# Three edits to the routed-expert stage of a one-core Trainium2 kernel: exchanged arms of a branch, another output place, an earlier split of inputs

## The chip, the cores and the metric

The kernel runs on one NeuronCore of a Trainium2 chip. The metric is device time in microseconds. The profiler's record of one execution is the trace read below. Engines are named as in the profile: PE (TensorE, matrix products), DVE (VectorE), ACT (ScalarE), POOL (GpSimd) and SP (the queue that issues most loads). Each engine runs its own list of instructions in order and waits on semaphores for the others.

## The reference, cut to what matters

Local and global attention gives 2176 rows of 512 numbers. A feed-forward stage with a squared relu follows, and then a stage of routed experts, the only one that the change touches:

```python
do_compute = x @ w_skip > 0
xc = x[do_compute]
e_idx = np.argmax(xc @ w_gate, axis=1)         # one of 8 experts
for e in range(E):                             # F = 1024, D = 512
    mask = e_idx == e
    h = np.maximum(xc[mask] @ w1[e], 0.0)
    y[mask] = gate_w[mask, None] * (h @ w2[e])
out[do_compute] = xc + y                       # other rows stay x
```

For the input that is timed, the experts 0 to 7 get 337, 24, 22, 433, 82, 126, 86 and 133 rows.

## The kernel before

Every float32 product is done as three products of a high and a low half (fp32r): weights and inputs are each split, the high half by ACT (a cast), the low half by DVE (a subtraction, line 846 for weights). In names like `e34h` and `e34l` the number is 8 times the expert plus the part of its weights, so `e32` to `e39` are expert 4's and `e40` to `e47` expert 5's.

The rows of one expert are worked in tiles of 128 (`expert_tile`), in eight steps with a `yield` after each: four of the first product (relu goes to `er`, is transposed and split into `ehl`), four of the second (into `y`), then the output `eo` on DVE (line 1061: gate times y plus x), then an indirect DMA on POOL that scatters the rows to `out` (line 1065). Inputs come by an indirect gather on POOL (`gather`, line 990), are transposed on PE (`etr`) and split (`prepare`).

How many tiles an expert has is known only at run time. Expert e's tile 0 always runs. Behind it, `more(e, 1)` holds further tiles under branches (line 1384). Experts 1 and 2 have so few rows here that they go together through a small path, and then `run(range(3, 8))` does experts 3 to 7. For expert 3 there is one question more: if its count needs exactly seven half tiles, the 305 rows behind tile 0 go through `wide_tile`, one tile of 320 columns, and otherwise through `more(3, 1)`. `prepare_wide` makes its inputs in three pieces (`etr_1w` to `etr_3w`, low halves on line 925), its first product is in lines 937 to 939, its outputs are transposed back (line 976), formed on DVE (line 982, three tiles `ewo`, `ewo` and `xg_wide`) and scattered on POOL (`scatter_rest`, line 1132). The other inputs of this run take the path so far described: expert 3 tile 0 and the wide tile, experts 4, 5 and 6 one tile each, expert 7 one tile and a rest of 32 rows.

The order on every engine is the order in which the code emits instructions. `run` calls `work(e, u)` after step u of expert e: it converts the next expert's weights by the table `PARTS_AT`, five parts ahead, issues loads of later weights, and by `AHEAD` two gathers, that of expert e+2's tile 0 after step 2 and that of expert e+1's further tile after step 3. `prepare(e, 1)` stands after step U1 = 5 and `prepare(e + 1, 0)` after step U0 = 6, whether or not the further tile turns out to be needed. Both scatter and gather go through POOL in program order, and a scatter to `out` waits for the scatter before it.

Places in SBUF go by tags. "xt" has one buffer: all `eo` tiles use it, and so do the first of the wide tile's outputs and the outputs of the small paths. "vgr" has one buffer, too, for values that attention reads; the expert stage did not use it. A new tile of a tag waits until all readers of the last one, a scatter among them, are done.

A branch can have a hint: `mark_branch_hint_location`, called after step 0 of the expert's tile 0, tells PE ahead whether the branch will be taken.

Of the kernel before, what the change touches and what calls it, by code (L numbers as in the profile page):

```python
# [54 lines left out]
def attention_ffn_routed_experts(  # L55
# [24 lines left out]
    SG = q_g.shape[2]  # L80
    P = 128
# [20 lines left out]
    BLK = 2 * P  # L102
# [12 lines left out]
    def sb(tag, bufs, shape, name, dtype=F32):  # L115
        return spool.tile(shape, dtype, tag=tag, bufs=bufs, name=name + arm[0])
# [267 lines left out]
    def load_v_global(b, g):  # L384
        h0 = 4 * g
        vgl[b, g] = stage(f"gv{b}_{g}").rearrange("p (h j d) -> p h j d", h=4, j=TPB)
        nc.sync.dma_start(vgl[b, g], v_l[b, h0:h0 + 4].rearrange("h (p j) d -> p h j d", j=TPB))
        if g == 0:
            vgr[b] = sb("vgr", 1, [SG, DM], f"vgr{b}")
            nc.sync.dma_start(heads(vgr[b]), v_g[b].rearrange("h s d -> s h d"))  # L390

    def attention(t, S_TAG, O_TAG):
# [416 lines left out]
    BEHIND = 5  # L809
    AHEAD = {2: ((2, 0),), 3: ((1, 1),)}  # L810
    PARTS_AT = {0: (0, 1), 1: (2,), 2: (3,), 3: (4,), 4: (5,), 5: (6,), 6: (7,)}
    U0, U1 = 6, 5
    FEW, AFTER = (1, 2), 3
    WIDE = 2 * P + P // 2
    raws, spare, shared = {}, [], {}
# [98 lines left out]
    def prepare_wide(e, j):  # L914

        n = P // 2 if j == 3 else P
        cols = slice((j - 1) * P, (j - 1) * P + n)
        tr = pair(f"etr_{e}_{j}w")
        transposes(tr, wide_x[e] if j == 3 else gathered(e, j), n)
        high, low = ([x[:, :, cols] for x in xs] for xs in wide_slices())  # L920
        for z in range(2):
            nc.scalar.copy(high[z], tr[:, 2 * z:2 * z + 2, 0:n])
        for l, h, k in ((low[0], high[0][:, 0:1], 0), (low[1], high[0][:, 1:2], 1), (low[2], high[1], 2)):
            w = l.shape[1]
            nc.vector.tensor_tensor(out=l, in0=tr[:, k:k + w, 0:n], in1=h.bitcast(F32), op=ALU.subtract)
# [82 lines left out]
    def expert_tile(e, j, si):  # L1008
# [48 lines left out]
        yield  # L1057
        second(6, KE)
        yield
        o = sb("xt", 1, [P, 3 * BLK], f"eo_{name}")[:, 0:DM]  # L1060
        nc.vector.scalar_tensor_tensor(
            out=o, in0=y, scalar=xg[:, DM:DM + 1], in1=xg[:, 0:DM], op0=ALU.mult, op1=ALU.add
        )
# [119 lines left out]
    with tc.manual_schedule():  # L1183
# [237 lines left out]
        def run(experts, later=(), ahead=NST - 1, late=U0):  # L1421
            later = list(later)
            for e in experts:
                for u, _ in enumerate(expert_tile(e, 0, slot(sidx, e, 0))):
                    if u in HINTS:
                        if is_wide(e):
                            tc.mark_branch_hint_location(f"wide{e}", hint=wide_count(e), engines=HINTS[u])
                        else:
                            hint(e, 1, HINTS[u])
                    if is_wide(e):  # L1430
                        if U1 <= u < U1 + 3:
                            prepare_wide(e, u - U1 + 1)
                    elif u == U1:
                        prepare(e, 1)
                        if e == E - 1:
                            prepare_rest(e, 1)
                    if u == (U0 if e != experts[0] else late) and e + 1 < E:
                        prepare(e + 1, 0)
                    work(e, u, ahead if e == experts[0] else NST - 1)
                    if later:  # L1440
                        later.pop(0)()
                if is_wide(e):
                    with tc.If(wide_count(e), label=f"wide{e}") as wide:  # L1443
                        wide_tile(e)
                    with wide.Else():
                        more(e, 1)
                else:
                    more(e, 1)

        def wide_count(e):  # L1450
            return (n_tok[e] + (P // 2 - 1)) // (P // 2) == 7

        more(0, 2)
        carried = dict(est), dict(raws)
# [78 lines left out]
```

## Time and profile before

| what | us |
|---|---|
| runs of the kernel before | 719.21, 726.43, 726.79 (median 726.43) |
| profiled execution | 724.18 |
| its span | 722.5 |
| PE busy in the span | 687.0 (95%) |
| DVE, ACT, POOL busy | 398.3, 368.7, 167.3 |
| expert 3, tile 0 on PE | 602.25 to 615.25 |
| wide tile on PE | 616.25 to 646.43 |
| experts 4, 5, 6, 7 on PE, first matmul | 649.43, 664.31, 681.25, 695.99 |
| rest of expert 7, first matmul | 709.15 |

The span is the profiled execution without its start and end. In rows of the timeline a number in square brackets is the time in which the engine stood idle before the instruction, with the name of what released it; a matmul's row gives its modelled length, so that the distance of two starts tells the pace. [...]

### The profile page before, as it was taken

To read this page: it belongs to the slowest core of one execution; us is meant where nothing else is said; L and a number is where in the kernel's file an instruction comes from. 1 tells how busy PE (TensorE), PEld (TensorE's weight loads), DVE (VectorE), ACT (ScalarE), POOL (GpSimd) and SP (SyncE) were. 2 spreads that over 40 slices of the span, in tenths; PEclk is the share of its full clock that TensorE was granted. 3 is DMA by queue.
4 is the path that set the end of the run, shared out by engine and by line. 5 is a ranking of instruction groups with operands and counts; after the bars stand their busy time and mean duration, and the time that the engine had idled before them with its cause. 6 is when DMAs were issued, how large, how long until landed. Compare 5 with 4: busy or idle time off the path is not lost. (4 is left out here: it accounts for less than half of the span.)

```text
span 722.5 us, 18733 instructions
## 1 busy us (share of the span) xinstructions
PE 687.0 (95%) x7617; PEld 576.4 (80%) x7617; DVE 398.3 (55%) x1073; ACT 368.7 (51%) x944; POOL 167.3 (23%) x209
## 2 busy tenths in 40 slices
PE   6789998999999999999999999999999999989995
PEld 4566677898888988988888898888878878987773
DVE  1889955763654265365245355525277428336882
ACT  5757567665534645544455363544345226226670
POOL 5000043472112221122112221122204235003211
PEclk8699999999999999999999999999999999999998
DMA  9999653064054304124620404010058599807800
GB/s 273 250 284 292 217 130 62 2 166 85 2 144 118 78 32 84 32 61 84 147 49 32 106 2 155 5 59 32 29 171 267 178 345 371 312 16 234 312 28 21
DMA packets 119096, 95.16 MB, mean 132 GB/s; under 512 B 84853, under 2 KB 92021, under 8 KB 118980
## 3 DMA queue, kind: packets, MB, share of 16 engines
q1 hardware_dynamic: 108352, 71.01, 34.9%
q10 hardware_dynamic: 8292, 15.48, 6.5%
q0 software_dynamic: 2336, 7.14, 2.9%
q8 instruction: 70, 1.15, 0.7%
q14 instruction: 46, 0.38, 0.2%
HBM read 81.36 MB, written 12.66 MB: 130 GB/s over the span
## 5 line engine op out<-in xcount | busy, mean ns | idle before, releaser
L184 POOL TENSOR_TENSOR gl<-g,gh 128x256 fp32r<-128x256 f32 x107 | 79.5, 743 | 302.6 <-ACT gh L183 153.6
L700 PE MATMUL h<-xh,w_in 128*128 128x256 f32 x464 | 134.8, 291 | 0.7 <-ACT xh L183 0.7
L701 PE MATMUL h<-xl,w_in 128*128 128x256 f32 x464 | 129.5, 279 | 0.3 <-DVE xl L184 0.3
L702 PE MATMUL h<-xh,w_in 128*128 128x256 f32 x464 | 129.7, 279 | 0.0
L725 PE MATMUL acc<-w_out,gh 128*128 128x512 f32 x232 | 97.6, 421 | 1.5 <-ACT gh L183 1.5
L727 PE MATMUL acc<-w_out,gl 128*128 128x512 f32 x232 | 91.8, 396 | 0.2
L726 PE MATMUL acc<-w_out,gh 128*128 128x512 f32 x232 | 91.6, 395 | 0.0
L700 PEld LDWEIGHTS h<-xh,w_in 128*128 128x128 f32 x464 | 87.1, 188 | 4.2 <-ACT xh L183 0.9
L701 PEld LDWEIGHTS h<-xl,w_in 128*128 128x128 f32 x464 | 87.2, 188 | 2.6 <-DVE xl L184 0.5
L704 ACT ACTIVATE g<-h 128x256 f32<-128x256 f32 x128 | 48.7, 381 | 77.0 <-PE h L702 45.1
L702 PEld LDWEIGHTS h<-xh,w_in 128*128 128x128 f32 x464 | 87.1, 188 | 0.0
L433 ACT ACTIVATE sm<-sm,mx 128x128 f32<-128x128 f32 x120 | 46.7, 390 | 50.1 <-DVE mx L431 50.1
L741 DVE TENSOR_TENSOR g<-h,g 128x256 f32<-128x256 f32 x53 | 22.2, 419 | 85.4 <-ACT g L704 85.3
L183 ACT CAST gh<-g 128x256 fp32r<-128x256 f32 x116 | 47.2, 407 | 42.8 <-DVE g L741 40.0
L727 PEld LDWEIGHTS acc<-w_out,gl 128*128 128x128 f32 x232 | 43.5, 188 | 11.9 <-POOL gl L184 1.5
L725 PEld LDWEIGHTS acc<-w_out,gh 128*128 128x128 f32 x232 | 43.6, 188 | 8.5 <-ACT gh L183 1.9
L726 PEld LDWEIGHTS acc<-w_out,gh 128*128 128x128 f32 x232 | 43.8, 189 | 5.7
L426 DVE TENSOR_TENSOR sm<-sc,mask 128x512 f32<-128x512 f32 x30 | 20.6, 687 | 24.2 <-PE sc L413 23.4
L255 POOL TENSOR_TENSOR w_in<-st_raw_in,w_in 128x512 fp32r<-128x512 f32 x10 | 13.0, 1308 | 81.4 <-ACT w_in L251 81.4
L413 PEld LDWEIGHTS sc<-kT,qT 64*32 64x32 f32 x2048 | 24.9, 108 | 5.2 <-issue 4.3
L990 POOL DMA_INDIRECT xg<-x2d,slots x15 | 20.6, 1371 | 36.5 <-DVE slots L800 13.1
L743 ACT ACTIVATE g<-g 128x256 f32<-128x256 f32 x63 | 26.2, 416 | 4.7 <-ACT g L704 2.5
(690 smaller groups left out, 1481.3 us busy)
## 6 DMA issues: line engine op xcount, KB each, us to landing
st_e<-in_moe_w_dram SPq DMA_DIRECT2D x46, 512.0 KB, 6.3
vr<-in_v_l_dram SPq DMA_DIRECT2D x49, 192.0 KB, 4.1
st_raw_in<-in_moe_w_in_dram SPq DMA_DIRECT2D x16, 512.0 KB, 7.1
st_raw_out<-in_moe_w_out_dram SPq DMA_DIRECT2D x16, 512.0 KB, 7.3
st_e<-in_moe_w_dram ACTq DMA_DIRECT2D x12, 512.0 KB, 5.4
x2d<-x ACTq DMA_DIRECT2D x19, 256.5 KB, 3.7
st_gv<-in_v_l_dram SPq DMA_DIRECT2D x8, 512.0 KB, 4.4
out_dram<-x ACTq DMA_DIRECT2D x16, 256.0 KB, 4.0
```

What stands on the lines that cost most here:

```text
L183: nc.scalar.copy(hi, src)
L184: (lo_engine or nc.vector).tensor_tensor(out=lo, in0=src, in1=hi.bitcast(F32), op=ALU.subtract)
L413: nc.tensor.matmul(scs[g][SEG * i:SEG * (i + 1), p, cols], lhsT=q[rows, p, SEG * i:SEG * (i + 1)], rhs=kT[b][rows, p, keys], start=True, s ...
L433: nc.scalar.activation(sm[:, hh, :], sm[:, hh, :], AF.Exp, bias=mx[:, hh:hh + 1], scale=SCALE, accum_out=osum[:, 2 * hh + g:2 * hh + g + 1],)
L700: nc.tensor.matmul(h, lhsT=wh, rhs=xh[:, k, :], start=(k == 0), stop=False)
L701: nc.tensor.matmul(h, lhsT=wh, rhs=xl[:, k, :], start=False, stop=False)
L702: nc.tensor.matmul(h, lhsT=wl, rhs=xh[:, k, :], start=False, stop=(k == KD - 1))
L704: nc.scalar.activation(g, h, AF.Relu)
L725: nc.tensor.matmul(acc[z], lhsT=gh[:, c], rhs=wh, start=first_one, stop=False)
L726: nc.tensor.matmul(acc[z], lhsT=gh[:, c], rhs=wl, start=False, stop=False)
L727: nc.tensor.matmul(acc[z], lhsT=gl[:, c], rhs=wh, start=False, stop=last_one)
L743: nc.scalar.activation(square, g, AF.Square)
```

## The change

It has three parts. The place of an expert's output: tile 0 of each expert puts it into the tag "vgr", which is allocated with 128 rows for that, and further tiles stay on "xt". The arms of expert 3's question: the question is turned round (`other_count`), so that `more(3, 1)` is the first arm and the wide tile the last; the hint is turned round with it. The preparation of the wide tile's inputs: it stands after the steps 4, 5 and 6 of expert 3's tile 0 instead of 5, 6 and 7.

```diff
--- before.py
+++ after.py
@@ -386,7 +386,7 @@
         vgl[b, g] = stage(f"gv{b}_{g}").rearrange("p (h j d) -> p h j d", h=4, j=TPB)
         nc.sync.dma_start(vgl[b, g], v_l[b, h0:h0 + 4].rearrange("h (p j) d -> p h j d", j=TPB))
         if g == 0:
-            vgr[b] = sb("vgr", 1, [SG, DM], f"vgr{b}")
+            vgr[b] = sb("vgr", 1, [P, DM], f"vgr{b}")[0:SG]
             nc.sync.dma_start(heads(vgr[b]), v_g[b].rearrange("h s d -> s h d"))
 
     def attention(t, S_TAG, O_TAG):
@@ -809,7 +809,7 @@
     BEHIND = 5
     AHEAD = {2: ((2, 0),), 3: ((1, 1),)}
     PARTS_AT = {0: (0, 1), 1: (2,), 2: (3,), 3: (4,), 4: (5,), 5: (6,), 6: (7,)}
-    U0, U1 = 6, 5
+    U0, U1, U2 = 6, 5, 4
     FEW, AFTER = (1, 2), 3
     WIDE = 2 * P + P // 2
     raws, spare, shared = {}, [], {}
@@ -1057,7 +1057,10 @@
         yield
         second(6, KE)
         yield
-        o = sb("xt", 1, [P, 3 * BLK], f"eo_{name}")[:, 0:DM]
+        if j:
+            o = sb("xt", 1, [P, 3 * BLK], f"eo_{name}")[:, 0:DM]
+        else:
+            o = sb("vgr", 1, [P, DM], f"eo_{name}")
         nc.vector.scalar_tensor_tensor(
             out=o, in0=y, scalar=xg[:, DM:DM + 1], in1=xg[:, 0:DM], op0=ALU.mult, op1=ALU.add
         )
@@ -1424,12 +1427,12 @@
                 for u, _ in enumerate(expert_tile(e, 0, slot(sidx, e, 0))):
                     if u in HINTS:
                         if is_wide(e):
-                            tc.mark_branch_hint_location(f"wide{e}", hint=wide_count(e), engines=HINTS[u])
+                            tc.mark_branch_hint_location(f"other{e}", hint=other_count(e), engines=HINTS[u])
                         else:
                             hint(e, 1, HINTS[u])
                     if is_wide(e):
-                        if U1 <= u < U1 + 3:
-                            prepare_wide(e, u - U1 + 1)
+                        if U2 <= u < U2 + 3:
+                            prepare_wide(e, u - U2 + 1)
                     elif u == U1:
                         prepare(e, 1)
                         if e == E - 1:
@@ -1440,15 +1443,15 @@
                     if later:
                         later.pop(0)()
                 if is_wide(e):
-                    with tc.If(wide_count(e), label=f"wide{e}") as wide:
+                    with tc.If(other_count(e), label=f"other{e}") as other:
+                        more(e, 1)
+                    with other.Else():
                         wide_tile(e)
-                    with wide.Else():
-                        more(e, 1)
                 else:
                     more(e, 1)
 
-        def wide_count(e):
-            return (n_tok[e] + (P // 2 - 1)) // (P // 2) == 7
+        def other_count(e):
+            return (n_tok[e] + (P // 2 - 1)) // (P // 2) != 7
 
         more(0, 2)
         carried = dict(est), dict(raws)
```

In the program, on PE, at the end of the wide arm (`ewtr` are its output transposes, `eh_1` further tiles of expert 3, `eh_0` with `e32h` expert 4), before:

```order
L976 MATMUL ewtr_1_a<-ident,ewys_a 128x128
L976 MATMUL ewtr_2_a<-ident,ewys_a 64x128
L1443 UNCONDITIONAL_BRANCH
L1384 COMPARE_AND_BRANCH
L1023 MATMUL eh_1_0_a<-e24h_a,xp_0_8022 128x512
L1024 MATMUL eh_1_0_a<-e24l_a,xp_0_8022 128x512
```

and in the change:

```order
L976 MATMUL ewtr_1_a<-ident,ewys_a 128x128
L976 MATMUL ewtr_2_a<-ident,ewys_a 64x128
L1446 UNCONDITIONAL_BRANCH
L1023 MATMUL eh_0_0_a<-e32h_a,xp_0_8020 128x512
L1024 MATMUL eh_0_0_a<-e32l_a,xp_0_8020 128x512
```

The wide arm lay before the block of `more(3, 1)`, and its unconditional branch jumped over that block to expert 4. Now expert 4 stands directly behind the branch. On PE the wide arm has 205 instructions in either program, and the other arm with its branch 365.

On PE, at the entry of the arms, behind the last product of expert 3's tile 0 (`etr_3w` and `etr_0_a` are transposes of the wide tile's last inputs and of expert 4's), before:

```order
L1040 MATMUL y_0_a<-e31h_a,ehl_0_a 128x512
L280 MATMUL etr_3w_a<-ident,xg_wide_a 128x64 x4
L280 MATMUL etr_0_a<-ident,xg_1_8016 128x128 x4
L1443 COMPARE_AND_BRANCH
L937 MATMUL ewh_0_a<-xp_0_8022,e24h_a 128x320
L938 MATMUL ewh_0_a<-xp_0_8022,e24h_a 128x320
L939 MATMUL ewh_0_a<-xp_0_8022,e24l_a 128x320
```

and in the change:

```order
L1039 MATMUL y_0_a<-e31l_a,ehl_0_a 128x512
L1040 MATMUL y_0_a<-e31h_a,ehl_0_a 128x512
L280 MATMUL etr_0_a<-ident,xg_1_8016 128x128 x4
L1446 COMPARE_AND_BRANCH
L1387 COMPARE_AND_BRANCH
L1023 MATMUL eh_1_0_a<-e24h_a,xp_0_8022 128x512
L1024 MATMUL eh_1_0_a<-e24l_a,xp_0_8022 128x512
```

Before, the wide tile (line 937) follows the branch; now `more(3, 1)` does, and the branch jumps over it to the wide tile. The transposes `etr_3w` have moved to a place ahead of the six matmuls of the last step.

On DVE, in the last steps of expert 3's tile 0 (`e31l` is the last part of expert 3's weights, `e32l` and `e33l` the first of expert 4's, `xp` the low halves of the wide tile's inputs), the piece of the difference between both programs, - for before and + for the change:

```order
-L846 TENSOR_TENSOR e31l_a<-st_e_8077,e31h_a 128x1024 [waits DMAHW0_49,DVE_49]
 L925 TENSOR_TENSOR xp_0_8022<-etr_1w_a,xp_0_8022 128x128 [waits PE_49,Activation_49]
 L925 TENSOR_TENSOR xp_0_8023<-etr_1w_a,xp_0_8022 128x128
 L925 TENSOR_TENSOR xp_1_8024<-etr_1w_a,xp_0_8023 128x2x128
-L846 TENSOR_TENSOR e32l_a<-st_e_8093,e32h_a 128x1024 [waits DMAHW1_49,DVE_49,Pool_49]
+L846 TENSOR_TENSOR e31l_a<-st_e_8077,e31h_a 128x1024 [waits DMAHW0_49,DVE_49]
 L925 TENSOR_TENSOR xp_0_8022<-etr_2w_a,xp_0_8022 128x128 [waits PE_49,Activation_49]
 L925 TENSOR_TENSOR xp_0_8023<-etr_2w_a,xp_0_8022 128x128
 L925 TENSOR_TENSOR xp_1_8024<-etr_2w_a,xp_0_8023 128x2x128
-L846 TENSOR_TENSOR e33l_a<-st_e_8232,e33h_a 128x1024 [waits DMAHW2_49,DVE_49]
+L846 TENSOR_TENSOR e32l_a<-st_e_8093,e32h_a 128x1024 [waits DMAHW1_49,DVE_49,Pool_49]
 L925 TENSOR_TENSOR xp_0_8022<-etr_3w_a,xp_0_8022 128x64 [waits PE_49,Activation_49]
```

Each group of three subtractions on line 925 stands one weight conversion sooner.

On DVE, at the output of expert 4's tile 0 (`eo_0_a`, read from `xg_1_8016`), with the queues that it waits for, before:

```order
L846 TENSOR_TENSOR e40l_a<-st_e_8174,e40h_a 128x1024 [waits DMAHW1_49]
L184 TENSOR_TENSOR xp_1_8021<-etr_0_a,xp_1_8021 128x512 [waits Activation_49]
L846 TENSOR_TENSOR e41l_a<-st_e_8381,e41h_a 128x1024 [waits DMAHW2_49]
L1061 SCALAR_TENSOR_TENSOR eo_0_a<-y_0_a,xg_1_8016 128x512 [waits DMASW3_49,DMASW4_49,DMASW2_49,DMASW5_49,DMASW1_49,DMASW7_49,DVE_49,PE_49]
L1384 COMPARE_AND_BRANCH
```

and in the change:

```order
L846 TENSOR_TENSOR e40l_a<-st_e_8174,e40h_a 128x1024 [waits DMAHW1_49]
L184 TENSOR_TENSOR xp_1_8021<-etr_0_a,xp_1_8021 128x512 [waits Activation_49]
L846 TENSOR_TENSOR e41l_a<-st_e_8381,e41h_a 128x1024 [waits DMAHW2_49]
L1064 SCALAR_TENSOR_TENSOR eo_0_a<-y_0_a,xg_1_8016 128x512 [waits DMASW5_49,DMASW1_49,PE_49]
L1387 COMPARE_AND_BRANCH
```

The waits for the queues DMASW3, DMASW4, DMASW2 and DMASW7, which carry the scatters of what lay in "xt", are gone; those for DMASW5, its own gather, and DMASW1 stay. On the path that runs here, the order of the scatters and gathers on POOL and their waits for one another are the same in both programs.

## Rows read from the trace of the kernel before

**Rows 1.** Page, its first line

```profile
span 722.5 us, 18733 instructions
```

**Rows 2.** Busy time by stretch, all engines; columns in the first line

```profile
core 0: us, PE busy (x) PEld busy (x) DVE busy (x) ACT busy (x) POOL busy (x), PEclk, DMA share, GB/s
649.43:653.00 3.57, 3.57 (x9) 2.79 (x10) 2.28 (x3) 0.00 (x0) 1.77 (x1) 0.52 0.61 184
664.30:681.25 16.95, 14.99 (x64) 11.66 (x65) 12.68 (x14) 11.20 (x15) 4.65 (x5) 0.90 0.94 315
...
695.99:709.15 13.16, 13.16 (x65) 10.43 (x65) 9.30 (x10) 7.82 (x11) 1.02 (x1) 1.00 0.06 18
```

**Rows 3.** PE's timeline at the wide tile's entry: start, us, instruction [idle <- releaser]

```profile
616.25 0.38 PE L937 MATMUL ewh_a<-xp,e24h_a 128*128 128x320 f32 x1
616.92 0.41 PE L938 MATMUL ewh_a<-xp,e24h_a 128*128 128x320 f32 x1 [0.29 <-DVE xp L925]
```

**Rows 4.** PE's timeline at the wide tile's exit

```profile
644.81 0.31 PE L958 MATMUL ewy_a<-ewgl_a,e31h_a 128*128 128x320 f32 x1
644.96 1.47 PE L976 MATMUL ewtr_a<-ident,ewys_a 128*128 128x128 f32 x12
649.43 0.73 PE L1023 MATMUL eh_a<-e32h_a,xp 128*128 128x512 f32 x1 [3.00 <-issue]
...
652.95 0.40 PE L1025 MATMUL eh_a<-e33h_a,xp 128*128 128x512 f32 x1
```

**Rows 5.** Branches on PE's sequencer by line: ns min/median/max, first and last start

```profile
L1443 PEldq COMPARE_BRANCH  x2: 83/1912/3742, 615.7 to 645.6; - x2
...
L1384 PEldq COMPARE_BRANCH  x7: 95/384/3751, 579.8 to 706.6; - x7
...
L1384 PEldq COMPARE_BRANCH  x1: 195/195/195, 593.1 to 593.1; - x1
```

**Rows 6.** PE's timeline in expert 5

```profile
664.31 0.47 PE L1023 MATMUL eh_a<-e40h_a,xp 128*128 128x512 f32 x1
...
666.25 0.40 PE L1025 MATMUL eh_a<-e41h_a,xp 128*128 128x512 f32 x1
...
669.38 0.50 PE L1024 MATMUL eh_a<-e42l_a,xp 128*128 128x512 f32 x1 [1.80 <-DVE e42l_a L846]
```

**Rows 7.** DVE's timeline behind the wide tile, in expert 5 and in expert 6

```profile
648.23 1.21 DVE L846 TENSOR_TENSOR e34l_a<-st_e,e34h_a 128x1024 fp32r<-128x1024 f32 x1
...
667.04 0.75 DVE L1061 SCALAR_TENSOR_TENSOR eo_a<-y_a,xg 128x512 f32<-128x512 f32 x1 [1.79 <-DMA out_dram<-xg_wide_a,slots]
668.10 1.23 DVE L846 TENSOR_TENSOR e42l_a<-st_e,e42h_a 128x1024 fp32r<-128x1024 f32 x1 [0.31 <-ACT er_a L1028]
...
683.16 1.23 DVE L846 TENSOR_TENSOR e50l_a<-st_e,e50h_a 128x1024 fp32r<-128x1024 f32 x1 [0.31 <-DVEq L1384]
```

**Rows 8.** POOL's timeline behind the wide tile

```profile
647.28 1.00 POOL L1132 DMA_INDIRECT out_dram<-ewo_a,slots  x1 [28.11 <-DVE ewo_a L982]
650.80 1.77 POOL L1132 DMA_INDIRECT out_dram<-ewo_a,slots  x1 [2.52 <-DVE e35l_a L846]
660.85 1.51 POOL L1132 DMA_INDIRECT out_dram<-xg_wide_a,slots  x1 [8.28 <-DVE ehl_a L184]
...
664.64 1.51 POOL L990 DMA_INDIRECT xg<-x2d,slots  x1 [0.30 <-issue]
```

**Rows 9.** DMA issues of two short windows (660.85, 664.64): us to landing last

```profile
out_dram<-xg_wide_a,slots POOLq DMA_INDIRECT x1, 5.9
...
xg<-x2d,slots POOLq DMA_INDIRECT x1, 7.9
```

**Rows 10.** PE's timeline in expert 6 and at expert 7's start

```profile
681.25 0.47 PE L1023 MATMUL eh_a<-e48h_a,xp 128*128 128x512 f32 x1
...
690.75 0.60 PE L280 MATMUL etr_a<-ident,xg 128*128 128x128 f32 x4
...
695.99 0.47 PE L1023 MATMUL eh_a<-e56h_a,xp 128*128 128x512 f32 x1 [1.42 <-PEq L1384]
```

## The prediction

> **What bounds the kernel now.** I read the page first: the span is 722.5 us [rows 1], and TensorE (PE) is busy for 95% of it, so only what makes PE stand still or run slowly can move the time. The profiled execution took 724.18 us, 1.7 us of it outside the span. The runs shown have a median of 726.43 and differ among themselves by 1%, so about 1% is what a measurement of this kernel can tell from no change. My sum is made against 724.18, which is 0.3% under that median and close to the mean of the numbers shown.
>
> Then I read PE's timeline around the lines of the diff, where PE loses time in three places.
>
> First, the exit of the wide tile. The last transposes end at 644.96 + 1.47 = 646.43 and the next matmul, expert 4's first, begins at 649.43: 3.00 us idle that no data explains [rows 4]. The branch of line 1443 at the end of the arm took PE's sequencer 3742 ns [rows 5]. It jumps over the whole block of the other arm, and no hint was given for it. [...]
>
> Second, inside expert 5. PE waits 1.80 us at 669.38 for `e42l` [rows 6]. VectorE (DVE) made it late because its previous instruction, expert 4's output on line 1061, had itself stood 1.79 us until the scatter of `xg_wide` landed [rows 7]: that output lies in the place "xt", like the wide tile's first output, and the wait takes in the wide tile's scatters. The clock falls again: 0.90 over the expert, which takes 16.95 us against 13.16 for expert 7 [rows 2]. Of these 3.79 us, I take 0.2 for the passage to the next expert, which stays, and 0.1 for the small wait that expert 6 has too; 3.5 hangs on the late `e42l`.
>
> Third, the entry of the wide tile. Its second matmul begins 0.67 us after its first, with 0.29 idle until the low half of the inputs is there [rows 3]; such matmuls otherwise stand 0.15 apart, as from 644.81 to 644.96 [rows 4]. That is 0.52 lost.
>
> **The change, part by part.**
>
> *Arms exchanged.* The wide arm now lies directly in front of expert 4, and its last branch goes to the next instruction. A short jump of an arm in this trace took 195 ns [rows 5]; the present exit hides 3.74 - 3.00 = 0.74 us because the sequencer runs ahead of PE, so what stays costs between 0 and 0.2; I take 0. The idle 3.00 and the slow 1.58 behind it go: 4.55, rounded. Is the data there so early? Expert 4's first half needs nothing new. The second needs `e34l`, which DVE makes from 648.23 behind the wide tile's outputs, for 1.21 us [rows 7]; with 0.5 less at the wide tile's entry it ends at 648.95. PE, starting at about 646.0, wants it 13 matmuls later at some 0.24 each, near 649. So 0 to 0.3 of a new wait; I take 0.
>
> The same exchange moves the price to the entry: what fell through now jumps over the other expert tiles. This jump has its hint, set one expert tile earlier. Of the seven branches of line 1384 on PE the median took 384 ns and only the longest 3751 [rows 5]; that one, in front of expert 7, had been hinted as well and left 1.42 us of idle time [rows 10] at full clock [rows 2]. At the wide tile's entry the sequencer is at the branch at 615.7 [rows 5] and the first matmul starts at 616.25 [rows 3]: a lead of 0.55. A hinted jump of 0.4 us fits into it: 0. A missed one shows 3.75 - 0.55 = 3.2 us as idle time, and with the 1.58 of the slow clock behind such a gap costs 4.8; were the lead that in front of expert 7, 1.42. I take 0, since the middle of these rows is a hit.
>
> [...]
>
> *An output place of its own.* Expert 4's output no longer waits for the wide tile's scatters, only for its own inputs and for expert 3's scatter, landed long ago. `e42l` then stands as in expert 6, where `e50l` began 683.16 - 681.25 = 1.91 us after the expert's first matmul instead of 668.10 - 664.31 = 3.79 [rows 6, 7, 10]. All 3.5 us go. Bounds: 3.3 (idle and slow clock without the small rests) to 3.8 (the whole difference). At expert 0's tiles and at the end of the kernel nothing waited for "xt", so nothing is gained there; the place "vgr" was last read by attention, long before.
>
> *Inputs split one step sooner.* Each of the three preparations moves up by one step, so on PE, ScalarE and DVE the same transposes, copies and subtractions stand in front of one weight conversion instead of behind it. The last low half is done about a micro-second sooner; the 0.52 at the entry goes. In exchange `e31l` to `e33l` each come up to 0.8 us later, but `e31l` is wanted behind two more groups of matmuls. Between 0 and 0.52 I take 0.5.
>
> *What is late next.* GpSimd (POOL) issues the wide tile's three scatters one after the other, each when the one before has landed: issues at 647.3, 650.80, 660.85 [rows 8]. Behind them in its program stand the two gathers of expert 4's steps, the second of which fetches the rows for expert 5's further tile: issued at 664.64 [rows 8], under way for 7.9 us [rows 9], so landed at 672.54. Nothing of that is changed but the start, 0.5 us sooner: it lands at 672.0. Were the scatters and gathers slowed by loads that come denser, it would be up to 1 us later; `xg_wide` took 5.9 [rows 9] with loads running already.
>
> PE wants these rows at expert 5's transposes. In expert 6 the same step stands at 690.75 - 681.25 = 9.50 us [rows 10]. Before, with its 3.5 us of losses, expert 5 came there at 664.31 + 9.50 + 3.5 = 677.3, far behind the landing; hence no wait shows today. After the change expert 5 starts at 664.31 - 4.55 - 0.5 = 659.26 and comes there at 668.76. PE stands 672.04 - 668.76 = 3.28 us. Its transposes are in program order ahead of the second half of expert 5's second product; on DVE and ScalarE the copies of these inputs hold up the later conversions equally, so nothing fills the gap. Both longer idle times of this trace (3.00 and 1.80) were followed by the 0.5 clock, the 1.42 was not [rows 2, 4, 6, 10]; so another 1.58 as above. This wait costs 4.85; bounds 0 (if the rows land 3.3 us sooner) and 5.8.
>
> Sum: -4.55 - 3.5 - 0.5 + 4.85 = -3.7, and 724.18 - 3.7 = **720.5 us**, 0.5% less. One can say it as a cap: whatever PE saves behind the wide tile, it cannot pass expert 5's transposes before 672.0 instead of 677.3, and pays 1.58 for standing there.
>
> **Rivals.**
>
> 1. *The new wait does not come.* The gather would have to land by 668.8. For it: the first scatter landed within 3.5 us (the second could start at 650.80 [rows 8]). Against it: under the loads the second took until shortly before 660.85, and the loads come no later than before. Then -8.55, 715.6 us, 1.2% faster.
>
> [...]
>
> 3. *The entry's jump misses.* The delay moves the wide tile's end and with it the scatters, so nothing absorbs it: 720.5 + 4.8 = 725.3, slower than before (with the 1.42 of expert 7, 721.9). For it: the jump spans the same block, and one of the hinted jumps missed. Against it: the others hit. It makes the change a loss from 3.7 us on.
>
> **How the numbers follow.** The forecast, with the new wait, has 0.55; rival 1 0.17; rival 2 0.06; rival 3 0.20, a quarter of that at the smaller price; 0.02 is left for what I don't see. The range leaves out about half of rival 1 and somewhat less than half of rival 3: 715.5 to 725.2; the forecast alone would be 718.9 (no slow clock behind the wait) to 721.7 (the gather 1 us later, and 0.3 for `e34l`). Faster by over 1% (under 716.9) is rival 1, and the runs' own spread lets some of the forecast fall there: 0.26. Slower by over 1% (above 731.4) needs more than rival 3: 0.06. The rest, 0.68, is within 1%.
>
> **What would show it.** In the profile after: expert 4's first matmul within 0.5 us of the wide tile's last transposes at clock 1.00; expert 4's output without a wait for `xg_wide`, and no idle time in front of `e42l`; no idle time at the second matmul of the wide tile; the entry's branch on PE at some 400 ns. And in expert 5, an idle time of about 3.3 us in front of the transposes of its further rows, released by a gather's DMA, with a clock of 0.5 behind it. The prediction is wrong if that gather lands much sooner behind the wide tile's last transposes than now (672.54 - 646.43 = 26.1 us; at 22.8 there is no wait), or if the entry's branch takes over 3 us.

## The result, and the profile after

The changed kernel took 717.3 us at the median of 5 runs (715.54 to 718.15), the kernel before 725.84 us (719.21 to 726.79, 5 runs). The ratio is 0.9893, with a 95% interval of 0.9846 to 0.9940. Two later measurements of the same kernel, each beside the kernel before on one chip, gave 0.9888 (0.9848 to 0.9928) and 0.9905 (0.9870 to 0.9940). So it is about 1% faster: inside the stated range, 3 us under the predicted 720.5 (and under the 718.9 to 721.7 that the forecast alone allowed), and on the border between the "within 1%" that I held likeliest and "faster by over 1%".

Three executions of the changed kernel have a profile. The stages on PE, by the start of their first matmul, in us:

| stage | before | changed, first profile | changed, second profile | changed, third profile |
|---|---|---|---|---|
| expert 3 begins at | 602.25 | 601.02 | 603.61 | 602.96 |
| expert 3, tile 0 | 14.00 | 13.95 | 13.95 | 13.95 |
| wide tile, to its output transposes | 28.71 | 28.15 | 28.15 | 28.15 |
| from there to expert 4 | 4.47 | 1.23 | 1.23 | 1.23 |
| expert 4 | 14.88 | 13.60 | 13.59 | 13.60 |
| expert 5 | 16.94 | 18.33 | 13.87 | 13.90 |
| expert 6 | 14.74 | 13.49 | 14.81 | 14.75 |
| span | 722.5 | 716.4 | 716.4 | 715.4 |
| profiled execution | 724.18 | 718.15 | 718.17 | 717.17 |

PE's timeline of the first of them at the wide tile's entry, at its exit, in expert 5 and at expert 7's start (start, us, instruction, idle time before it and what ended it):

```profile
614.97 0.39 PE L937 MATMUL ewh_a<-xp,e24h_a 128*128 128x320 f32 x1
615.20 0.31 PE L938 MATMUL ewh_a<-xp,e24h_a 128*128 128x320 f32 x1
...
643.12 1.47 PE L976 MATMUL ewtr_a<-ident,ewys_a 128*128 128x128 f32 x12
644.35 0.48 PE L1023 MATMUL eh_a<-e32h_a,xp 128*128 128x512 f32 x1
...
670.75 1.09 PE L280 MATMUL etr_a<-ident,xg 128*128 128x128 f32 x4 [3.13 <-DMA xg<-x2d,slots]
...
689.77 0.47 PE L1023 MATMUL eh_a<-e56h_a,xp 128*128 128x512 f32 x1
```

At the entry the second matmul now follows without idle time (0.29 in [rows 3]). At the exit expert 4 begins as the transposes end (3.00 in [rows 4]). In expert 5 the idle time has another place: not in front of `e42l` [rows 6] but in front of the transposes of the expert's further rows, 3.13 us, ended by the landing of a gather. In front of expert 7 the 1.42 us of [rows 10] are missing.

DVE in expert 5, the rows that answer to [rows 7]:

```profile
658.80 0.74 DVE L1064 SCALAR_TENSOR_TENSOR eo_a<-y_a,xg 128x512 f32<-128x512 f32 x1
659.86 1.23 DVE L846 TENSOR_TENSOR e42l_a<-st_e,e42h_a 128x1024 fp32r<-128x1024 f32 x1 [0.31 <-DVEq L1387]
```

Expert 4's output no longer waits, and `e42l` begins 659.86 - 657.95 = 1.91 us after expert 5's first matmul, the figure of expert 6 before.

The branches on PE's sequencer (ns min/median/max, first and last start), as in [rows 5]; the first is the new jump at the entry:

```profile
L1446 PEldq COMPARE_BRANCH  x1: 448/448/448, 613.2 to 613.2; - x1
...
L1387 PEldq COMPARE_BRANCH  x7: 92/368/579, 578.5 to 700.6; - x7
```

The stretches of experts 4, 5 and 6 (length, busy time of each engine, the clock granted to PE as a share of the full one, DMA share), as in [rows 2]:

```profile
644.35:657.95 13.60, 13.42 (x68) 10.43 (x65) 12.96 (x15) 10.38 (x14) 2.98 (x3) 1.00 0.71 232
657.95:676.28 18.33, 15.05 (x65) 11.56 (x65) 12.58 (x14) 11.09 (x15) 8.83 (x6) 0.91 0.91 311
676.28:689.77 13.49, 13.34 (x65) 10.43 (x65) 12.60 (x14) 11.11 (x15) 3.27 (x3) 1.00 0.34 115
...
670.70:675.00 4.30, 4.25 (x16) 3.60 (x17) 1.82 (x2) 1.75 (x3) 0.89 (x1) 0.61 0.82 313
```

Expert 4 runs at full clock (1.00). Expert 5 loses time twice, by the wait and by the clock of 0.61 in the stretch behind it (0.50 from 671.5 to 673.5).

The second and third profile differ from the first at that place. PE's timeline in the second, then in the third:

```profile
669.82 0.40 PE L1040 MATMUL y_a<-e45h_a,ehl_a 128*128 128x512 f32 x1
670.40 0.63 PE L280 MATMUL etr_a<-ident,xg 128*128 128x128 f32 x4 [0.19 <-DMA xg<-x2d,slots]
...
689.21 0.47 PE L1023 MATMUL eh_a<-e56h_a,xp 128*128 128x512 f32 x1 [1.47 <-PEq L1387]
```

```profile
669.79 0.63 PE L280 MATMUL etr_a<-ident,xg 128*128 128x128 f32 x4 [0.23 <-DMA xg<-x2d,slots]
```

The same wait is there, but it is 0.2 us long, and no slow clock follows (1.00 over expert 5 in both). Instead the jump in front of expert 7 is long again (1.3 us more in expert 6), and expert 3 begins 2.6 and 1.9 us later. That all three spans lie within 1 us is therefore chance: different things went wrong in each.

### The profile page after: what moved, and what is told of

It reads as the page before. It is cut to its first block, busy times and chain, and to the rows that moved or that the text cites. A ratio compares the mean times of both kernels' runs of the same rounds, so it can differ in the third digit from the quotient of the medians.

```text
span 716.4 us, 18721 instructions
## 1 busy us (share of the span) xinstructions
PE 686.0 (96%) x7617; PEld 575.5 (80%) x7617; DVE 398.5 (56%) x1073; ACT 368.3 (51%) x944; POOL 169.2 (24%) x209
## 5 line engine op out<-in xcount | busy, mean ns | idle before, releaser
L426 DVE TENSOR_TENSOR sm<-sc,mask 128x512 f32<-128x512 f32 x30 | 20.6, 688 | 23.3 <-PE sc L413 22.5
L990 POOL DMA_INDIRECT xg<-x2d,slots x15 | 21.9, 1459 | 38.2 <-DVE slots L800 13.1
L743 ACT ACTIVATE g<-g 128x256 f32<-128x256 f32 x63 | 26.2, 416 | 4.4 <-ACT g L704 3.4
```

Of the source, the lines that this page charges most:

```text
L743: nc.scalar.activation(square, g, AF.Square)
```

## The experiments

Twelve runs follow: nine variants, one of them run twice, and the changed kernel twice more. In the expectations, A says that the serial scatters on POOL set when PE can go on in expert 5, B that each part gains its own stall independently, D that the loads of weights decide and that a transfer brought forward makes another late. The parts come first, each alone on the kernel before, on one chip. The diffs show the lines that matter; "..." stands for the lines between them.

**Only the arms exchanged.**

```diff
-    with tc.If(wide_count(e), label=f"wide{e}") as wide:
-        wide_tile(e)
-    with wide.Else():
-        more(e, 1)
+    with tc.If(other_count(e), label=f"other{e}") as other:
+        more(e, 1)
+    with other.Else():
+        wide_tile(e)
...
-        def wide_count(e):
-            return (n_tok[e] + (P // 2 - 1)) // (P // 2) == 7
+        def other_count(e):
+            return (n_tok[e] + (P // 2 - 1)) // (P // 2) != 7
```

> Only the arms of expert 3's question are exchanged; outputs stay in one place and the inputs are split as before. Theory A (the scatters behind the wide tile set the time at which PE can go on in expert 5): expert 4 starts about 4.5 us sooner, but its output still waits for the landing of xg_wide at about 666.7, e42l is ready at 669.3 as before, and PE stands some 6.4 us in front of it instead of 1.8. Time as before, ratio 1.000 (within 0.2%). Theory B (each part gains its own stall, independently): 4.55 us less, ratio 0.9937. A missed jump in front of expert 7 can add or take 1.4 us in either.

Measured: ratio 0.9992 (0.9977 to 1.0006). DVE's timeline in expert 5, then PE's, then the stretch of expert 5 as in [rows 2]:

```profile
664.86 0.75 DVE L1061 SCALAR_TENSOR_TENSOR eo_a<-y_a,xg 128x512 f32<-128x512 f32 x1 [4.80 <-DMA xg<-x2d,slots]
```

```profile
667.21 0.80 PE L1024 MATMUL eh_a<-e42l_a,xp 128*128 128x512 f32 x1 [4.82 <-DVE e42l_a L846]
```

```profile
659.12:679.50 20.38, 15.41 (x65) 12.02 (x65) 12.68 (x14) 11.21 (x15) 5.33 (x6) 0.83 0.85 293
```

The exit's 4.5 us are gained (1.23 to expert 4, 13.60 for expert 4 at clock 1.00), and then, 3.4 of them in this execution, handed to the next wait: 4.82 us in front of `e42l` where there were 1.80, and 20.38 us for expert 5 where there were 16.94. The largest of the three savings is worth nothing alone. That is theory A; B is out. The first row names a gather as releaser, but the gather issued at 659.95 landed only 6.0 us later, at 665.95, when the output had begun; what its wait fits is the scatter of `xg_wide`, issued at 658.39 (5.9 us to landing in [rows 9]), and with the output in a place of its own this wait is gone (next run). It is 1.6 us shorter than I said, because the second scatter took 8.26 us to the third instead of 10.05; that comes back below.

**Only the output's own place.**

```diff
-            vgr[b] = sb("vgr", 1, [SG, DM], f"vgr{b}")
+            vgr[b] = sb("vgr", 1, [P, DM], f"vgr{b}")[0:SG]
...
-        o = sb("xt", 1, [P, 3 * BLK], f"eo_{name}")[:, 0:DM]
+        if j:
+            o = sb("xt", 1, [P, 3 * BLK], f"eo_{name}")[:, 0:DM]
+        else:
+            o = sb("vgr", 1, [P, DM], f"eo_{name}")
```

> Only the output place of an expert's first tile is its own. Both theories: the idle 1.8 us in front of e42l and the slow clock behind it go, 3.5 us less, ratio 0.9952; the exit of the wide tile keeps its 3.0 us and its slow clock. Theory A: expert 5 comes to the transposes of its further rows at about 673.8, after their landing at 672.5, so no wait shows there. Theory C (the own place gains nothing, since e42l waits for something else too): ratio 1.000.

Measured: ratio 0.9962 (0.9934 to 0.9990). Experts 4 and 5:

```profile
649.80:664.67 14.87, 14.72 (x64) 11.69 (x65) 10.13 (x12) 9.08 (x12) 4.60 (x4) 0.89 0.72 234
664.67:678.13 13.46, 13.31 (x64) 10.44 (x65) 12.57 (x14) 11.10 (x15) 3.23 (x4) 1.00 1.02 356
```

Expert 4 has its slow clock as before; expert 5 takes 13.46 us instead of 16.94: 3.48 less, as said, and no wait for the further rows shows, since PE comes to them late enough. 3.5 us is 0.9952, which the interval holds. C is out.

**Only the earlier split.**

```diff
-    if U1 <= u < U1 + 3:
-        prepare_wide(e, u - U1 + 1)
+    if U1 - 1 <= u < U1 + 2:
+        prepare_wide(e, u - U1 + 2)
```

> Only the wide tile's inputs are split one step sooner. Theory A and B: the second matmul of the wide tile follows its first without idle time, 0.5 us less behind it, and all scatters and waits move with it: ratio 0.9993, not to be told from 1. Theory C: the weight conversions that now come later (e31l to e33l) make PE wait before the wide tile, ratio 1.000 or above.

Measured: ratio 0.9981 (0.9960 to 1.0001), which says nothing on half a micro-second. The profile does, for one execution: the wide tile takes 28.15 us to its output transposes instead of 28.71, and expert 3's tile 0 in front of it 13.95 instead of 14.00, so the later weight conversions delay nothing.

**Arms and place, without the earlier split** (the two diffs above together).

> Arms exchanged and own place, without the earlier split. Theory A: expert 5's wait for its further rows is there as in the changed kernel (3.1 us, for PE and the scatters both start 0.5 us later); 0.5 us more than the changed kernel, ratio to before 0.9955 by the steps. Theory B (parts independent): 4.55 + 3.5 less, ratio 0.989.

Measured: ratio 0.9916 (0.9885 to 0.9947), beside 0.9888 for the changed kernel on the same chip: 718.2 us against 717.36. Alone, arms and place make 0.08% and 0.38%; together 0.84%. The arms' gain is real as soon as the output's place no longer hands it on. The interval holds B's 0.989 and not A's 0.9955, so on the number A missed. The profile says why: the wait for the further rows that A expects is there, but with 0.58 us of idle time and no slow clock (1.00) it cost only 14.25 - 13.48 = 0.8 us.

**The wait in expert 5 taken away.** This starts from the changed kernel. The two gathers of expert 4's steps (expert 6's first tile, expert 5's further rows) are issued ahead of the wide tile's scatters:

```diff
+        gather_ahead(e)
         for t, o in enumerate(os):
             scatter_rest(o, slot(sidx, e, t + 1)[0:o.shape[0]])
+
+    def gather_ahead(e):
+        for n, j in ((3, 0), (2, 1)):
+            gather(e + n, j, slot(gidx, e + n, j))
...
-                if e + n < E:
+                if e + n < E and not (e == AFTER + 1 and arm[0] == "_a"):
                     gather(e + n, j, slot(gidx, e + n, j))
```

> The changed kernel, and the two gathers of expert 4's steps (expert 6's first tile, expert 5's further rows) are issued on POOL ahead of the wide tile's three scatters instead of behind them. Theory A (the wait of 3.13 us in expert 5 comes from POOL's order, gathers behind scatters that wait for one another): expert 5's rows land by about 652, the wait and the slow clock behind it go, 4.85 us less than the changed kernel: about 712.5 us, ratio to before 0.982. Theory D (the gather is late because loads fill the DMA queues at that time): it lands sooner, but another transfer takes its place (the scatters, then the gathers of expert 6), and the time stays within 1.5 us of the changed kernel, ratio 0.988.

Measured: ratio 0.9977 (0.9951 to 1.0003), worse than the changed kernel; 720.87 to 727.47 us, and the profile, 726.74, is of one of the slower executions. POOL's timeline behind the wide tile, experts 5 and 6, and DVE and PE in expert 6:

```profile
648.35 1.02 POOL L995 DMA_INDIRECT xg<-x2d,slots  x1 [26.33 <-DVE ewo_a L982]
649.67 4.02 POOL L1140 DMA_INDIRECT out_dram<-ewo_a,slots  x1 [0.30 <-issue]
660.41 1.01 POOL L1140 DMA_INDIRECT out_dram<-ewo_a,slots  x1 [6.72 <-DVE e40l_a L846]
668.70 1.68 POOL L1140 DMA_INDIRECT out_dram<-xg_wide_a,slots  x1 [7.28 <-DVE e45l_a L846]
676.00 0.99 POOL L1073 DMA_INDIRECT out_dram<-eo_a,slots  x1 [5.62 <-DVE e49l_a L846]
```

```profile
660.87:674.34 13.47, 13.32 (x65) 10.44 (x65) 12.57 (x14) 11.10 (x15) 2.23 (x2) 1.00 1.01 360
674.34:697.01 22.67, 15.42 (x64) 11.99 (x65) 14.28 (x15) 11.26 (x16) 6.91 (x6) 0.85 0.30 100
```

```profile
680.44 0.75 DVE L1069 SCALAR_TENSOR_TENSOR eo_a<-y_a,xg 128x512 f32<-128x512 f32 x1 [5.16 <-DMA out_dram<-eo_a,slots]
```

```profile
682.79 0.80 PE L1029 MATMUL eh_a<-e50l_a,xp 128*128 128x512 f32 x1 [5.18 <-DVE e50l_a L846]
```

On the wait A is right: expert 5 runs at full pace, 13.47 us. On the time D is right in kind, another transfer became late, though 5 us is far more than the 1.5 that it allowed. One gather of 1 us ahead of the first scatter moved that scatter's issue from 645.44 - 644.59 = 0.85 us behind the wide tile's transposes to 649.67 - 647.51 = 2.16. Its issue then took 4.02 us, and it was under way for 10 us instead of some 3; that the loads, which begin at about that time, are the reason is argued and not shown. Every later scatter came later by that much, and expert 5's output, in the same place as expert 4's, waited 5.16 us for expert 4's scatter. It is the old stall, one expert further on.

**The gather in the gap.** POOL stands idle for 2.51 us between the issues of the first scatter and the second in the changed kernel's first profile. So expert 5's gather goes there, behind the first scatter, and expert 6's stays ahead of it; expert 4's steps issue neither:

```diff
+        gather(e + 3, 0, slot(gidx, e + 3, 0))
         for t, o in enumerate(os):
             scatter_rest(o, slot(sidx, e, t + 1)[0:o.shape[0]])
+            if t == 0:
+                gather(e + 2, 1, slot(gidx, e + 2, 1))
```

> The changed kernel with expert 6's gather ahead of the wide tile's scatters and expert 5's gather right behind the first of them, where POOL stands idle for 2.5 us and the loads of weights have not begun. Theory A' (POOL's serial scatters, each of which takes 8 to 10 us once loads run, set the cap; what stands behind a scatter issued under the loads is late): expert 5's rows land by about 651, the 3.1 us wait and the slow clock behind it go, the scatters keep their times within 1 us, and expert 4's scatter lands by 671, in time for expert 5's output at 671.5: 4.85 us less than the changed kernel measured beside it, about 712.5 us. Theory D (the loads decide: whatever is taken from PE's wait comes back one transfer later): expert 5's output waits 2 us or more for expert 4's scatter, which lies in the same place, and the gain is under 2 us.

Measured: ratio 0.9919 (0.9886 to 0.9952), 718.34 us with executions from 716.11 to 721.99; the changed kernel beside it 717.36. In the profile (716.11 us, the quickest of the seven) expert 5 takes 13.47 us. But the median is no better. With the outputs of experts 5 and 7 in the old place in addition,

```diff
-        if j:
+        if j or e % 2:
             o = sb("xt", 1, [P, 3 * BLK], f"eo_{name}")[:, 0:DM]
```

> As gather_between, and the outputs of experts 5 and 7 lie in the old place again, so that no output waits for the scatter of the expert before it. Theory A': the same time as gather_between if its output of expert 5 did not wait, else better by that wait; 712.5 us. Theory D: expert 6's gathers, behind expert 4's scatter in POOL's order, land after 681, and PE waits for them in expert 6 instead; 715 us or more.

it was 0.9939 (0.9915 to 0.9962), 716.32 to 722.55 us. Both miss their 712.5. In time that is D (under 2 us gained), but the waits that D names are short in the two profiles: expert 5's output waits 0.28 us in the first and 0.68 in the second, both times, by the row, for expert 4's scatter, so the other place did not free it. Each has a profile of its quickest execution only; where the others lost time is not shown. In the profile of the second, PE begins expert 6 at 671.77, 4.5 us sooner than in the changed kernel's first profile, while the gathers for experts 6 and 7 are issued at 674 and 675 only:

```profile
666.24 1.65 POOL L1071 DMA_INDIRECT out_dram<-eo_a,slots  x1 [5.13 <-DVE e45l_a L846]
674.01 1.05 POOL L993 DMA_INDIRECT xg<-x2d,slots  x1 [6.12 <-DMA out_dram<-eo_a,slots]
675.36 1.20 POOL L993 DMA_INDIRECT xg<-x2d,slots  x1 [0.31 <-issue]
```

POOL waited 6.12 us until expert 4's scatter had landed, before it issued the gather. So the next link of the same chain was a candidate.

**The scatter behind the gathers.** As gather_between; besides, the scatter of an expert's first tile is issued behind the next expert's two gathers, and experts 5 and 7 put their outputs into a third place:

```diff
+        elif e > AFTER and e % 2:
+            o = sb("pT", 2, [P, 4, P], f"eo_{name}").rearrange("p a k -> p (a k)")
...
+        if AFTER < e < E - 1 and j == 0:
+            held.append((o, si))
+        else:
+            scatter_rest(o, si)
...
                 work(e, u, ahead if e == experts[0] else NST - 1)
+                if u == 3 and held:
+                    scatter_rest(*held.pop())
```

> As gather_between, and the scatter of an expert's first tile (experts 4 to 6) is issued behind the two gathers of the next expert's steps instead of ahead of its branch; outputs of experts 5 and 7 lie in a third place. Theory A' (what remained in gather_between's slower executions is POOL's order: expert 6's further rows are fetched behind expert 4's scatter and its landing): those gathers are issued near 668 instead of 675 to 677, land 5 us before expert 6 wants them, and the executions come close to gather_between's best, 716 us at the median with the missed jump in front of expert 7, 1.5 us under the changed kernel. Theory D (the loads take the DMA engines whatever POOL's order is): rows still land too late in some executions and the median stays at 717.5 or more.

Measured: 714.99 us, ratio 0.9886 (0.9851 to 0.9921), executions from 713.71 to 716.74. Its POOL behind the wide tile, and experts 5 and 6:

```profile
660.13 0.93 POOL L1142 DMA_INDIRECT out_dram<-xg_wide_a,slots  x1 [6.72 <-DVEq L1394]
666.92 1.14 POOL L993 DMA_INDIRECT xg<-x2d,slots  x1 [5.86 <-PE ertr_a L280]
668.36 1.71 POOL L993 DMA_INDIRECT xg<-x2d,slots  x1 [0.30 <-issue]
670.38 1.56 POOL L1142 DMA_INDIRECT out_dram<-eo_a,slots  x1 [0.30 <-issue]
```

```profile
658.43:671.90 13.47, 13.32 (x65) 10.44 (x65) 12.58 (x14) 11.11 (x15) 5.30 (x4) 1.00 1.01 367
671.90:686.33 14.43, 13.33 (x64) 10.42 (x65) 13.55 (x15) 11.16 (x16) 2.10 (x3) 1.00 0.47 151
```

The gathers are issued 7 us sooner, both experts run at clock 1.00, and the executions spread over 3 us instead of 6. The ratio is that of the changed kernel on another chip, so both ran once more side by side:

> The changed kernel, beside late_scatter on one chip. Theory A' : ratio to before 0.989 as measured twice, and in its profile the wait in expert 5 is somewhere between 0.4 and 4.5 us, by how long the second of the wide tile's scatters was under way (7.4 us in the profile with almost no wait, 8.8 in the one with 3.1).

> late_scatter once more, beside the changed kernel on one chip. Theory A': experts 5 and 6 at full pace in every execution, 1.5 to 2.5 us under the changed kernel (ratio to before 0.9865). Theory D: the same time as the changed kernel within 1 us.

Measured there: the changed kernel 717.88 us, ratio 0.9905 (0.9870 to 0.9940); late_scatter 715.72 us, 0.9872 (0.9837 to 0.9907). Its profile there is of its slowest execution, 717.38, and has experts 5 and 6 at clock 1.00 too (13.49 and 14.95 us). Four of its six executions (714.33 to 716.01) lie below the quickest of the changed kernel (716.04). So by 2.2 us at the median it is the best version here, as A said; the intervals of the two ratios against the kernel before overlap. What the third place for outputs gives without the later scatter was not run; the old place for every other output, the run before, gave nothing. The changed kernel's profile there is the third of the table above. Its wait in expert 5 cost 13.90 - 13.48 = 0.4 us, the lower end of what was expected, although the second scatter took 8.06 us to the third, between the 7.4 and the 8.8: that time alone does not set the wait.

**The changed kernel once more**, because my sum was 3 us too long:

> The changed kernel once more, beside the others on their chip. If the 2.6 us by which it was quicker than my sum are chance (where the beginning happened to be 1.2 us quicker and the jump in front of expert 7 happened to be fast), ratio to before 0.994 to 0.995 and a profile in which these two differ from the first; if they belong to the change, 0.989 again with a fast jump in front of expert 7 and expert 3's first matmul near 601.0.

Measured: 717.36 us, ratio 0.9888. The profile is the second of the table above. Neither of the two explanations on record holds as written: the ratio stayed, and yet the beginning was 2.6 us later and the jump in front of expert 7 long again. What had become shorter was the wait in expert 5.

**The hints given later.** This asks what the missed jump at the entry (the third rival) would have cost, and whether a hint's lead matters:

```diff
-    HINTS = {0: ENGINES[:1]}
+    HINTS = {4: ENGINES[:1]}
```

> The changed kernel, with every hint of this stage given after step 4 of the expert's first tile instead of step 0, so some 5 us ahead of its branch instead of 11. Theory H (a hint given long ahead is lost again while PE's sequencer passes through the code between): the jump in front of expert 7 takes about 0.4 us like the others, 1.4 us less in the executions that had it long (all profiles but one), 716.2 us. Theory I (the long jump in front of expert 7 has another cause): it stays between 2.3 and 4.4 us in the profile and the time is that of the changed kernel, 717.4. Theory J (a later hint is too late): other jumps become long as well, the wide tile's entry loses 3 us with the slow clock behind it, 721 us or more.

Measured: 727.48 us, ratio 1.0060 (1.0035 to 1.0085), some 10 to 12 us more than the changed kernel on the other chips. That is theory J; the jump in front of expert 7 took 3.58 us, so H is out. The branches on PE's sequencer, then PE at the wide tile's entry and at expert 5's start:

```profile
L1446 PEldq COMPARE_BRANCH  x1: 4461/4461/4461, 616.9 to 616.9; - x1
L1387 PEldq COMPARE_BRANCH  x7: 95/3582/5045, 581.5 to 708.7; - x7
```

```profile
621.49 0.39 PE L937 MATMUL ewh_a<-xp,e24h_a 128*128 128x320 f32 x1 [2.61 <-issue]
...
667.03 0.47 PE L1023 MATMUL eh_a<-e40h_a,xp 128*128 128x512 f32 x1 [2.71 <-PEq L1387]
```

The jumps at the entry and in front of expert 5, 4461 and 5045 ns, are no shorter than that of the unhinted exit, 3742 ns [rows 5]. With the hint at step 0, in the first profile, the same two took 448 and 352 ns. What a long jump waits for no trace here shows.

## Why the prediction was right, and where it was not

*The exit of the wide tile*: right to 0.03. Predicted 4.55; the way to expert 4 is 4.47 - 1.23 = 3.24 shorter, expert 4 itself 14.88 - 13.60 = 1.28. The 1.58 of the slow clock in the prediction is from the trace of before: expert 4's first nine starts stretched over 652.95 - 649.43 = 3.52 us [rows 4] at a granted clock of 0.52 [rows 2], those of expert 5 over 666.25 - 664.31 = 1.94 [rows 6]. No wait for `e34l` shows. Rival 2, with 0.06, was that the exit keeps its 3.00 us of idle time; expert 4 begins as the transposes end, so it is out.

*The entry's jump*: the hinted jump took 448 ns and left no idle time, so rival 3 did not come. Its price was too high, though: a jump missed there showed 2.61 us of idle time, and the wide tile behind it ran at full pace (28.15 us), so some 2.9 us (16.80 for expert 3's tile and the gap, against 13.95) and not 4.8, in the one execution that shows it.

*The own place*: right; 3.48 against 3.5, measured alone.

*The earlier split*: right; 0.56 against 0.5.

*What is late next*: the mechanism was right, in its place, its releaser and, in the first profile, its size: 3.13 us of idle time against 3.28, and with the slow clock 18.33 - 13.48 = 4.85 against 4.85 (13.47 to 13.49 is an expert at full pace). From expert 3's start to expert 6's the first profile is 79.00 - 75.26 = 3.74 us shorter, where I had summed 3.7. That this profile agrees so closely is luck, as the other two show.

*Where it failed* is the sentence "Nothing of that is changed but the start, 0.5 us sooner: it lands at 672.0". It took the times of the scatters and gathers from the kernel before. From the end of the wide tile's transposes to the end of the wait in expert 5 the three profiles have 670.75 - 644.59 = 26.2, 670.40 - 647.18 = 23.2 and 669.79 - 646.53 = 23.3 us, and arms_and_place has 23.6. I had read 26.1, and written that at 22.8 there is no wait. POOL in the first profile, then in the second, the rows that answer to [rows 8]:

```profile
648.96 1.78 POOL L1135 DMA_INDIRECT out_dram<-ewo_a,slots  x1 [2.51 <-DVE e35l_a L846]
657.75 1.92 POOL L1135 DMA_INDIRECT out_dram<-xg_wide_a,slots  x1 [7.02 <-DVE xp L184]
...
662.31 1.94 POOL L990 DMA_INDIRECT xg<-x2d,slots  x1 [0.30 <-issue]
```

```profile
651.55 1.78 POOL L1135 DMA_INDIRECT out_dram<-ewo_a,slots  x1 [2.51 <-DVE e35l_a L846]
658.92 1.50 POOL L1135 DMA_INDIRECT out_dram<-xg_wide_a,slots  x1 [5.59 <-DVE xp L184]
...
662.70 1.87 POOL L990 DMA_INDIRECT xg<-x2d,slots  x1 [0.30 <-issue]
```

The same times in all profiles whose POOL order is that of the kernel before, in us:

| profile | second scatter to third | DMA share between them | transposes' end to the gather for expert 5 |
|---|---|---|---|
| before | 10.05 | 0.68 | 18.21 |
| only the place | 9.20 | 0.68 | 16.65 |
| only the split | 9.57 | 0.68 | 17.92 |
| only the arms | 8.26 | 0.88 | 15.55 |
| arms and place | 7.95 | 0.87 | 15.52 |
| changed, three profiles | 8.79, 7.37, 8.06 | 0.95, 0.94, 0.86 | 17.72, 15.52, 15.53 |
| later hints | 8.27 | 0.87 | 15.57 |

Every profile with the arms exchanged has a shorter second scatter than every one without, six profiles against three, so this is hardly spread alone: it looks as if the exchange moved the chain itself. It certainly moved the loads: the fourth load behind the transposes is issued after 652.11 - 644.59 = 7.5 us, in the kernel before after 658.47 - 646.43 = 12.0. The loads are denser and the scatter is nevertheless quicker, against what I feared; why is not shown. The spread comes on top: one profile in six has 17.7 us to the gather, the others 15.5.

So the term of 4.85 was 4.85 in one profile and 0.4 in the other two (13.87 and 13.90 for expert 5). With 0.4 the sum is -8.15, 716.0 us and 0.9887, which is close to rival 1, and the three measured ratios are 0.9888 to 0.9905. I gave rival 1 0.17 and should have given it at least as much as the forecast. The median lies in the range because the range took in half of rival 1.

*The rest of the first profile's 6.0 us* comes from places that the change doesn't touch: expert 3 began 1.23 us sooner, and the jump in front of expert 7 took 579 ns instead of 3751, 1.25 us less in expert 6. Expert 3's start lies between 601.0 and 604.7 in the profiles of this study, and the jump was long again in both later profiles.

How often in unprofiled executions the wait in expert 5 is long is not shown.

## What to carry to other kernels

A stall that is taken away moves PE up to the next thing that is timed by somebody else; here a chain of serial transfers on POOL did the timing, so three savings were worth 0.08%, 0.38% and 0.19% alone (the first and the last cannot be told from nothing) and 1.1% together. Walk down that chain before summing: where does each of its members land, and who asks for it how soon after the change. And do not take a transfer's time under load from one execution of the kernel before: it varies from execution to execution (the second scatter to the third took 8.79, 7.37 and 8.06 us in three of the changed kernel), and here it was shorter in every profile with the arms exchanged (7.37 to 8.79 us) than without (9.20 to 10.05). A wait worked out as the difference of such a chain and PE's arrival turns from 3 us to nothing on 3 us of that chain.

## What the runs showed of the hardware

A late branch hint did not help here. In the first profile of the changed kernel the hints at step 0 came 11.3 to 13.1 us ahead of their branches at the entry and in front of experts 5 and 6, and the jumps took 352 to 475 ns; given 3.5 to 4.9 us ahead they took 4.46, 5.05 and 4.06 us, no less than the unhinted exit's 3.74 [rows 5]. The jump in front of expert 7, with 10.7 us of lead in the changed kernel, was nevertheless long in every profile of the study but one (2.3 to 4.4 us against 0.58). In gathers_first the lead was 18.0 us and the jump took 4.41, so it is not a matter of lead alone; why is open.

Some 3 us of idle time do not always bring the slow clock. Behind 2.61 us at the wide tile's entry with late hints the clock stayed at 1.00 (from 621.49 to 626.00); behind 2.71 in front of expert 5 in the same execution it was 0.51 (668.3 to 671.0), and behind the 3.13 above and behind 1.80 before [rows 6] it fell to 0.50.

A scatter of 128 rows from POOL landed within 2.8 us when no loads ran, and took 7.3 when they did (DMA share 1.00 from 651.56 to 658.8); DMA issues of late_scatter in two short windows (us to landing last):

```profile
out_dram<-ewo_a,slots POOLq DMA_INDIRECT x1, 2.8
...
out_dram<-ewo_a,slots POOLq DMA_INDIRECT x1, 7.3
```

The first was issued at 645.93, ahead of the loads, the second at 651.56, among them.
